# Attention woven into a feed-forward network: ten small pieces a step, all in program order, with new Gram blocks and an inversion over three steps

## The chip, the cores and the metric

The kernel runs on one core of one Trainium2 chip, all in fp32. The metric is device time in microseconds (us); the kernel before takes 770.18 us (median of three runs, 769.65 to 772.47). Engines are named as the profile names them: PE is TensorE's matmuls, PEld its weight loads, DVE is VectorE, ACT is ScalarE, POOL is GpSimd, SP issues the DMAs. A line such as L571 is a line of the kernel that the profile belongs to, so the same operation has another line number in another version; a small table below gives both.

## The reference

Two blocks in a row: a delta-rule attention over 768 positions, and a feed-forward network with a PReLU in the middle.

```python
# q, k, v: (4, 8, 768, 48), beta: (4, 8, 768)
k_n = k / (norm(k) + 1e-6)
for t in range(S):
    y[:, :, t] = q_t @ state
    state = state + beta_t * outer(k_t, v_t - k_t @ state)
x = y.transpose(0, 2, 1, 3).reshape(3072, 384)
h = x @ w_in                                  # 384 -> 2048
g = maximum(h, 0) + alpha * minimum(h, 0)
out = g @ w_out                               # 2048 -> 384
```

The kernel cuts the 768 positions into 12 chunks of 64, and the four batch entries into two pairs, so there are 24 attention steps `n`. In a chunk the recurrence becomes a triangular system per head. Its 64x64 inverse is made from two 32x32 blocks, which VectorE inverts, and two small products on TensorE (`between_1`, `between_2`). The entries of the system come from Gram matrices, the products of a chunk's k with itself and with its q, for which k and q are transposed first (`flips`).

## The kernel before

VectorE inverts the blocks of four steps at once (`eliminate`: 30 pairs of a product and an addition, then two transposes of the whole block). A step of attention has four pieces, and `weave` deals the pieces out among the feed-forward products. PSUM is the memory that TensorE writes its results to. "Filler" is products whose results nobody needs, which keep TensorE busy where it would wait.

```python
BUSY = 31        # filler products ahead of the first groups that need an inverse
EARLY = 6        # Gram matrices are made this many steps ahead

def ps_big():    # three buffers of two PSUM banks, for all attention
    return psum.tile([128, 2, 512], FP32, name="p_big", tag="big", bufs=3)
def ps_one():    # half of such a buffer
    return ps_big()[:, 0]
def ps_ffn():    # two buffers of one bank, for all feed-forward products
    return psum.tile([128, 512], FP32, name="p_ffn", tag="ffn", bufs=2)

def flips(n_k, n_q):                       # transposes of k and of q
    both = n_k < N and n_q < N
    p = ps_big() if both else None         # one tile, two halves
    if n_k < N:
        p_k = p[:, 0] if both else ps_one()
        flip(early(n_k), p_k)              # four TensorE transposes
        ...
        nc.scalar.copy(k_t[n_k]..., p_k)
    if n_q < N:
        p_q = p[:, 1] if both else ps_one()
        flip(q_pad[n_q % NQ], p_q)
        ...
        nc.scalar.copy(q_t[n_q]..., p_q)

def eliminate(m):                          # blocks of steps 4m to 4m + 3
    ...
    for j in range(1, HB - 1):             # 30 pairs on VectorE
        nc.vector.tensor_tensor(out=prod, ..., op=ALU.mult)
        nc.vector.tensor_tensor(out=r[...], in0=r[...], in1=prod, op=ALU.add)
        yield
    nc.vector.transpose(turned[m]..., r)
    nc.vector.transpose(inverse[m]..., r...)
    yield

def attention(n):                          # four pieces
    place(n + 1)                           # ScalarE puts the blocks into diag and inv
    through_state(n)
    yield
    solve(n)
    yield
    outputs(n)                             # and the next state
    between_1(n + 1)
    grams(n + EARLY, n + 1)
    yield
    between_2(n + 1)
    to_ffn(n)
    flips(n + EARLY + 1, n + 2)
    prep(n + EARLY + 1)
    ...                                    # loads of later steps
    yield

# opening, in program order (a manual schedule on all engines): weights, steps 0 to 3
busy(BUSY)
...
weave((eliminate(1), HB), (ffn_out(0, True), OUT_PARTS))
place(NJ); between_1(NJ); between_2(NJ); grams(N, NJ); scale_v(NJ)
opening.close()                            # from here on a scheduler orders the engines

for n in range(NJ, N):
    gens = [(attention(n), 4)]
    if (n + 2) % NJ == 0 and n + 2 < N:
        gens.append((eliminate((n + 2) // NJ), HB))   # a whole inversion in one step
    ...                                    # half a chunk of feed-forward products
    weave(*gens)
```

A feed-forward product is two instructions on TensorE in the profile, a group of 16 quarter-array products of attention is 32 instructions, and a "visit" below is an uninterrupted stretch of attention work between two stretches of feed-forward work.

## Time and profile before

| | before |
|---|---|
| median time | 770.18 us |
| span of the profiled run, granted clock | 767.8 us, 0.982 |
| TensorE busy | 721.8 us, 94% |
| first output product of the feed-forward network | at 150.5 us |
| last one ends (start of its last instruction and 0.32 us) | at 763.4 us |

After 150.5 us TensorE sets the pace. The two costliest rows of the groups of instructions are these (busy time and mean length of one, then the idle time of the engine just before them and what ended the largest part of it):

```profile
L571 PE MATMUL p_ffn<-xt,w_in 128*128 128x256 f32 x1152 | 275.1, 391 | 14.1 <-DVE g L582 6.9
L601 PE MATMUL p_ffn<-w_out,g 128*128 128x384 f32 x768 | 262.2, 494 | 3.8 <-ACT diag L439 2.9
```

TensorE is idle before its wide products for only 14.1 + 3.8 us of 767.8, and what ended the largest part of that (6.9 us) is `g`, the eviction on VectorE (L582).

Line numbers of the operations that are named most:

| operation | before | after |
|---|---|---|
| feed-forward in / out | L571 / L601 | L593 / L623 |
| evict `g` on VectorE | L582 | L604 |
| transposes of k and q (`flips`) | L323 | L327 |
| copy k transposed out of PSUM (`k_t`) | L337 | L341 |
| `between_1`, `between_2` | L463, L476 | L480, L495 |
| filler | L663 | L697 |

### The profile page before, as it was taken

The numbers are of one execution on the slowest core, as the hardware profiler recorded it, in microseconds if no ns is written. First come the engines' busy times: TensorE is split into PE (matmuls) and PEld (weight loads), VectorE is DVE, ScalarE is ACT, GpSimd is POOL, SyncE is SP. The second block draws the span as 40 slices with busy tenths as digits, with TensorE's granted clock in tenths as the row PEclk, the third lists the DMA queues.
The fourth block names the chain that finished last, engine by engine and source line by source line (L and its number), as shares of the span: only waits on it lengthen the run. The fifth ranks groups of instructions, "written<-read, shape, count | busy, mean of one in ns | idle before, by whom it ended". The sixth has DMA issues, their size and how long they took to land.

```text
span 767.8 us, 20517 instructions
## 1 busy us (share of the span) xinstructions
PE 721.8 (94%) x8987; PEld 517.9 (67%) x8987; DVE 412.2 (54%) x979; ACT 251.7 (33%) x563; POOL 21.5 (3%) x80
## 2 busy tenths in 40 slices
PE   5999888898998999998999998999999999999997
PEld 4546666555676678666678667678667677687774
DVE  5886788896599224596224596214596233132020
ACT  3416656514424234125134124123114223021110
POOL 5000000010000000000000000000000000000000
PEclk9999899999999999999999999999999999999999
DMA  6815564311321122121122121111111110100000
GB/s 120 215 39 144 136 175 99 81 25 32 64 47 31 30 43 43 23 42 34 31 43 44 22 43 22 33 32 32 22 33 33 22 35 10 22 12 2 21 0 21
DMA packets 110185, 37.61 MB, mean 49 GB/s; under 512 B 103392, under 2 KB 106480, under 8 KB 110096
## 3 DMA queue, kind: packets, MB, share of 16 engines
q1 hardware_dynamic: 110064, 36.29, 21.7%
q8 instruction: 71, 1.16, 0.6%
q14 instruction: 18, 0.15, 0.1%
q10 hardware_dynamic: 32, 0.01, 0.0%
HBM read 31.56 MB, written 4.72 MB: 47 GB/s over the span
## 4 chain that ended last, share of the span: by engine, by line
PE 57%; DVE 29%; ACT 6%; issue 6%; POOL 1%; DMA 1%; SPq 0%; POOLq 0%; DVEq 0%; ACTq 0%
PE p_ffn L601 24%; PE p_ffn L571 21%; DVE prod L413 7%; DVE block L419 7%; DVE g L582 2%; PE p_big L503 2%; PE p_big L353 2%; PE p_big L530 2%; PE p_big L517 1%; DVE block L399 1%; DVE turned L424 1%; ACT diag L439 1%; DVE inverse L426 1%; DVE kk L359 1%; PE p_big L536 1%
## 5 line engine op out<-in xcount | busy, mean ns | idle before, releaser
L571 PE MATMUL p_ffn<-xt,w_in 128*128 128x256 f32 x1152 | 275.1, 391 | 14.1 <-DVE g L582 6.9
L601 PE MATMUL p_ffn<-w_out,g 128*128 128x384 f32 x768 | 262.2, 494 | 3.8 <-ACT diag L439 2.9
L571 PEld LDWEIGHTS p_ffn<-xt,w_in 128*128 128x128 f32 x1152 | 215.6, 193 | 50.0 <-ACT space_out L202 5.5
L601 PEld LDWEIGHTS p_ffn<-w_out,g 128*128 128x128 f32 x768 | 143.5, 192 | 95.9 <-ACT diag L439 3.2
L582 DVE SCALAR_TENSOR_TENSOR g<-low,al_t,p_ffn 128x256 f32<-128x256 f32 x192 | 83.6, 477 | 127.2 <-ACT low L579 127.1
L579 ACT ACTIVATE low<-p_ffn 128x512 f32<-128x512 f32 x96 | 56.8, 593 | 96.5 <-PE p_ffn L571 88.5
L413 DVE TENSOR_TENSOR prod<-block 128x30 f32<-128x30 f32 (+9 forms) x180 | 59.3, 330 | 5.5
L419 DVE TENSOR_TENSOR block<-block,prod 128x30 f32<-128x30 f32 (+9 forms) x180 | 59.4, 330 | 5.1
L544 DVE TENSOR_TENSOR y<-y,p_big 128x384 f32<-128x384 f32 x22 | 12.1, 552 | 58.8 <-PE p_big L530 58.8
L607 ACT COPY o_sb<-p_ffn 128x384 f32<-128x384 f32 x24 | 11.5, 478 | 90.1 <-PE p_ffn L601 90.1
L663 PE MATMUL p_ffn<-k_t,ident 128*128 128x512 f32 x76 | 37.9, 647 | 0.0
L439 ACT ACTIVATE diag<-inverse,which 64x128 f32<-64x128 f32 (+1 forms) x72 | 28.7, 399 | 23.1 <-PE p_big L476 17.5
L467 ACT COPY mid<-p_big 128x256 f32<-128x256 f32 x24 | 8.8, 372 | 80.1 <-PE p_big L463 80.1
L506 DVE TENSOR_TENSOR r<-v_raw,p_big 128x384 f32<-128x384 f32 x22 | 12.0, 550 | 37.0 <-PE p_big L503 36.8
L481 DVE TENSOR_TENSOR inv<-inv,p_big 128x256 f32<-128x256 f32 x24 | 10.0, 417 | 37.2 <-PE p_big L476 36.5
L439 ACT ACTIVATE inv<-inverse,which 128x256 f32<-128x256 f32 x48 | 21.7, 500 | 24.7 <-PE p_big L517 24.5
L663 PEld LDWEIGHTS p_ffn<-k_t,ident 128*128 128x128 f32 x76 | 14.8, 204 | 16.2 <-issue 15.7
L439 ACT ACTIVATE diag<-turned,which 128x256 f32<-128x256 f32 x24 | 11.6, 506 | 39.5 <-DVE turned L424 39.4
L353 PE MATMUL p_big<-k_t 48*64 48x64 f32 x768 | 18.3, 239 | 6.2 <-ACT k_t L337 4.3
L476 PEld LDWEIGHTS p_big<-diag,mid 64*64 64x64 f32 x768 | 14.3, 141 | 13.7 <-issue 9.8
L306 DVE TENSOR_REDUCE norm<-ksq 128x8 f32<-128x384 f32 x24 | 13.1, 546 | 17.1 <-ACT ksq L304 17.1
L392 ACT ACTIVATE same<-kk,which 128x256 f32<-128x256 f32 x24 | 12.2, 508 | 29.5 <-DVE kk L359 29.4
(94 smaller groups left out, 634.6 us busy)
## 6 DMA issues: line engine op xcount, KB each, us to landing
w_out<-in_moe_w_in_dram SPq DMA_DIRECT2D x12, 512.0 KB, 5.5
qp<-in_q_dram SPq DMA_DIRECT2D x48, 96.0 KB, 2.9
v_raw<-in_v_dram SPq DMA_DIRECT2D x48, 96.0 KB, 2.8
kl<-in_k_dram SPq DMA_DIRECT2D x96, 48.0 KB, 2.7
out_dram<-o_sb SPq DMA_DIRECT2D x48, 96.0 KB, 2.2
ke<-in_k_dram SPq DMA_DIRECT2D x46, 96.0 KB, 3.0
space_out<-in_moe_w_out_dram SPq DMA_DIRECT2D x11, 384.0 KB, 3.7
w_out<-in_moe_w_out_dram SPq DMA_DIRECT2D x5, 384.0 KB, 3.7
```

The costliest lines, as they stand in the source:

```text
L353: nc.tensor.matmul(p[half(t ^ a if w else t), a, w, g], k_t[n][dims(a), g, half(t)], rhs[n][dims(a), g, half(t)],)
L413: nc.vector.tensor_tensor(out=prod, in0=r[:, 0:j, j : j + 1].to_broadcast([128, j, n]), in1=r[:, j : j + 1, j + 1 : HB].to_broadcast([128, ...
L419: nc.vector.tensor_tensor(out=r[:, 0:j, j + 1 : HB], in0=r[:, 0:j, j + 1 : HB], in1=prod, op=ALU.add)
L439: nc.scalar.mul(dst[n % NE][to or rows, a.start * G : a.stop * G, cols], src[m][rows, heads], which[rows, i : i + 1],)
L476: nc.tensor.matmul(p[half(t), a, g], mid[n % 2][half(t ^ a), a * G + g], diag[n % NE][half(t ^ a), a * G + g, HB:C],)
L503: nc.tensor.matmul(p[half(t), a, w, g], x[n][dims(a), g, half(t)], state[bp][dims(a), t, g])
L530: nc.tensor.matmul(p[half(t), a, g], a_t[n][half(t ^ a), a * G + g], us[n][half(t ^ a), a, g])
L571: nc.tensor.matmul(p_h[:, i], w_in[:, t, (f + i) * 128 : (f + i + 1) * 128], xt[:, t], start=(t == 0), stop=(t == KT - 1),)
L579: nc.scalar.activation(low, p_h, ACT.Relu, scale=-1.0)
L582: nc.vector.scalar_tensor_tensor(out=g[:, i], in0=low[:, i], scalar=al_t[:, f + i : f + i + 1], in1=p_h[:, i], op0=ALU.mult, op1=ALU.add,)
L601: nc.tensor.matmul(p_o[bp], gs[f // 2][:, f % 2, bp * 128 : (bp + 1) * 128], w_out[:, f], start=(f == 0), stop=(f == FT - 1),)
L663: nc.tensor.matmul(p, ident, k_t[NJ - 1].rearrange("p g i -> p (g i)"))
```

## The change

The intent is to keep TensorE always supplied: cut a step of attention into ten pieces, so that between two pieces there is a wide product to hide each hop over another engine; spread an inversion over three steps, so that VectorE is never full; make Gram matrices eight steps ahead; and fix the order of every engine by hand for the whole kernel, not for the opening alone.

```diff
-EARLY = 6
+EARLY = 8
+FIRST = 6
-    opening = ExitStack()
-    opening.enter_context(tc.manual_schedule(engines={
+    ctx.enter_context(tc.manual_schedule(engines={
...                                            # grams: kk and two masked gathers become
-            nc.vector.tensor_tensor(out=kk[n_k]..., in0=p[:, :, 0], in1=..., op=ALU.mult)
+            for dst, cols in (                 # two scaled evictions and two copies of 32 rows
+                (gather(n_k), slice(0, HB)), (right[n_k % EARLY][:, 1:], slice(HB, C))
+            ):
+                nc.vector.tensor_tensor(out=dst..., in0=p[:, :, 0, :, cols], in1=w, op=ALU.mult)
...
+    def changes(n):                            # steps up to 4 need fewer placements
+        return n > NJ
...
+    SHARES = 10
     def attention(n):
-        place(n + 1)
+        place(n + 1, (0,))
         through_state(n)
         yield
+        between_1(n + 1)
+        place(n + 1, (1, 2))
+        yield
         solve(n)
         yield
-        outputs(n)
-        between_1(n + 1)
-        grams(n + EARLY, n + 1)
-        yield
-        between_2(n + 1)
-        to_ffn(n)
         flips(n + EARLY + 1, n + 2)
         prep(n + EARLY + 1)
...
+        yield
+        outputs(n)
+        yield
+        between_2(n + 1)
+        scale_v(n + 1)
+        yield
+        next_state(n)
+        yield
+        grams(N, n + 1)
+        yield
+        grams(n + EARLY, N)
+        yield
+        to_ffn(n)
         yield
...
-    opening.close()
...
-        gens = [(attention(n), 4)]
-        if (n + 2) % NJ == 0 and n + 2 < N:
-            gens.append((eliminate((n + 2) // NJ), HB))
+        gens = [(attention(n), SHARES)]
+        if n == NJ:                            # two more Gram matrices, to be eight ahead
+            gens.append((catch_up(), 5 * (EARLY - FIRST) // 2))
+        if n == NJ + 1 or (n % NJ == 0 and NJ + 4 <= n < N - NJ):
+            blocks = eliminate(n // NJ + 1)
+        if n > NJ and n % NJ < 3 and n < N - NJ:
+            share = HB // 2 if n < 2 * NJ else 11
+            gens.append((part(blocks, share), share))
```

More of the change, by code (lines that the diff above doesn't have):

```diff
@@ L290 @@
         nc.gpsimd.memset(t, 0.0)
-    stats, k_t, q_t, kk, a_t = {}, {}, {}, {}, {}
+    right = [const.tile([128, H + 1, HB], FP32, name=f"right{i}") for i in range(EARLY)]
+    for t in right:
+        nc.gpsimd.memset(t[:, 0], 0.0)
+    stats, k_t, q_t, a_t = {}, {}, {}, {}
     def by_parity(x):
@@ L357, in grams @@
         if n_k < N:
-            kk[n_k] = work.tile([128, H, C], FP32, name="kk", bufs=EARLY)
-            nc.vector.tensor_tensor(
-                out=kk[n_k].rearrange("p (a g) i -> p a g i", a=2),
-                in0=p[:, :, 0],
-                in1=stats[n_k][1][:, 0:2, :, None].to_broadcast([128, 2, G, C]),
-                op=ALU.mult,
-            )
+            w = stats[n_k][1][:, 0:2, :, None].to_broadcast([128, 2, G, HB])
+            for dst, cols in (
+                (gather(n_k), slice(0, HB)), (right[n_k % EARLY][:, 1:], slice(HB, C))
+            ):
+                nc.vector.tensor_tensor(
+                    out=dst.rearrange("p (a g) i -> p a g i", a=2), in0=p[:, :, 0, :, cols],
+                    in1=w, op=ALU.mult,
+                )
             keep(n_k)
@@ L385, with gather @@
     same, block, inverse, turned = {}, {}, {}, {}
-    def keep(n):
+    def gather(n):
         m, j = n // NJ, n % NJ
@@ L391, in keep @@
             same[m] = work.tile([128, NJ, H, HB], FP32, name="same", bufs=1)
-        nc.scalar.mul(same[m][:, j], kk[n][:, :, 0:HB], which[:, 0:1])
-        nc.vector.scalar_tensor_tensor(
-            out=same[m][:, j], in0=kk[n][:, :, HB:C], scalar=which[:, 1:2], in1=same[m][:, j],
-            op0=ALU.mult, op1=ALU.add,
-        )
+        return same[m][:, j]
+    def keep(n):
+        m, j = n // NJ, n % NJ
+        for t in range(2):
+            own = slice(64 * t + HB, 64 * t + C)
+            if n < NJ:
+                nc.vector.tensor_copy(out=same[m][own, j], in_=right[n % EARLY][own, 1:])
+            else:
+                nc.scalar.copy(same[m][own, j], right[n % EARLY][own, 1:])
         if j == NJ - 1:
@@ L446, in place @@
         if 1 in parts:
-            put(diag, second, inverse, 1, a=slice(0, 1))
-            for t in range(2):
-                put(diag, second, inverse, 1, half(t), half(1 - t), slice(1, 2))
+            put(diag, second, inverse, 1, a=slice(0, 1 if changes(n) else 2))
+            if changes(n):
+                for t in range(2):
+                    put(diag, second, inverse, 1, half(t), half(1 - t), slice(1, 2))
         if 2 in parts:
             put(inv, first, inverse, 0)
-            put(inv, second, inverse, 1)
+            if changes(n):
+                put(inv, second, inverse, 1)
             w = stats[n][1]
@@ L463, in between_1 @@
             nc.tensor.matmul(
-                p[half(t ^ a), a, g], kk[n][half(t), a * G + g],
+                p[half(t ^ a if changes(n) else t), a, g],
+                right[n % EARLY][half(t), a * G + g : a * G + g + 2].rearrange("p b i -> p (b i)"),
                 diag[n % NE][half(t), a * G + g, 0:HB],
@@ L475, in between_2 @@
         for g, a, t in quarters():
+            x = half(t ^ a if changes(n) else t)
             nc.tensor.matmul(
-                p[half(t), a, g], mid[n % 2][half(t ^ a), a * G + g],
-                diag[n % NE][half(t ^ a), a * G + g, HB:C],
-            )
-        to = inv[n % NE].rearrange("p (a g) i -> p a g i", a=2)[:, :, :, HB:C]
-        nc.vector.tensor_tensor(out=to, in0=to, in1=p, op=ALU.add)
+                p[half(t), a, g], mid[n % 2][x, a * G + g], diag[n % NE][x, a * G + g, HB:C]
+            )
+        to, own = (
+            x[n % NE].rearrange("p (a g) i -> p a g i", a=2)[:, :, :, HB:C] for x in (inv, diag)
+        )
+        nc.vector.tensor_tensor(out=to, in0=to if changes(n) else own, in1=p, op=ALU.add)
     nv, rhs_, ys, us, xts = {}, {}, {}, {}, {}
@@ L532, in outputs @@
             )
-        if c < NCH - 1:
-            p_s = ps_big()[:, :, 0 : G * D].rearrange("p t (g d) -> p t g d", g=G)
-            for g, a, t in quarters():
-                nc.tensor.matmul(
-                    p_s[half(a), t, g], k_late[n % NKL][half(t ^ a), 2 * g + a],
-                    us[n][half(t ^ a), a, g],
-                )
         if c == 0:
@@ L546, in outputs, with next_state @@
             )
+    def next_state(n):
+        c, bp = steps[n]
         if c < NCH - 1:
-            nc.vector.tensor_tensor(out=state[bp], in0=state[bp], in1=p_s, op=ALU.subtract)
+            p = ps_big()[:, :, 0 : G * D].rearrange("p t (g d) -> p t g d", g=G)
+            for g, a, t in quarters():
+                nc.tensor.matmul(
+                    p[half(a), t, g], k_late[n % NKL][half(t ^ a), 2 * g + a],
+                    us[n][half(t ^ a), a, g],
+                )
+            nc.vector.tensor_tensor(out=state[bp], in0=state[bp], in1=p, op=ALU.subtract)
     def to_ffn(n):
@@ L651, in attention @@
         load_v(n + 3)
-        load_late(n + 2)
-        scale_v(n + 1)
+        yield
[5 more added lines that the diff above has]
+        next_state(n)
+        load_late(n + 2)
+        yield
[4 more added lines that the diff above has]
+        to_ffn(n)
         yield
@@ L676, in pair @@
             outputs(i)
+            next_state(i)
             load_late(i + 2)
@@ L794 @@
         (conv_out, PARTS_OUT - 10), (ffn_in(1), IN_PARTS),
-        (statics(2 * NJ, EARLY + 3), 2 * (EARLY + 4 - 2 * NJ) + 1),
+        (statics(2 * NJ, FIRST + 3), 2 * (FIRST + 4 - 2 * NJ) + 1),
     )
-    flips(EARLY + NJ, NJ)
+    flips(FIRST + NJ, NJ)
     flips(N, NJ + 1)
-    prep(EARLY + NJ)
-    load_early(EARLY + NJ + NKE)
+    prep(FIRST + NJ)
+    load_early(FIRST + NJ + NKE)
     load_q(NJ + 2)
@@ L813, in feed_forward, with catch_up @@
             yield from ffn_out(c)
+    def catch_up():
+        for n in range(FIRST + NJ, EARLY + NJ):
+            grams(n, N)
+            prep(n + 1)
+            flips(n + 1, N)
+            load_early(n + 1 + NKE)
+            yield
     tail = feed_forward()
```

## The prediction

> **What bounds the kernel now.** I read the page first: engine shares, the 40 slices, then the costly groups.
>
> ```profile
> PE 721.8 (94%) x8987; PEld 517.9 (67%) x8987; DVE 412.2 (54%) x979; ACT 251.7 (33%) x563; POOL 21.5 (3%) x80
> ...
> PE   5999888898998999998999998999999999999997
> ...
> DVE  5886788896599224596224596214596233132020
> ...
> PEclk9999899999999999999999999999999999999999
> ```
>
> TensorE (PE) is busy 94% of a span of 767.8 us, and from slice 12 on it is nearly always at 9. VectorE (DVE) is heavy in the opening and then in waves: a `596`-like crest every six slices, when a batch of blocks is inverted (180 pairs of products and additions at 330 ns each, 59.3 + 59.4 us in all, plus transposes of 2 us). So after the opening TensorE sets the pace, except on the crests. The end of the chain of waits gives TensorE's undisturbed rate for the two feed-forward products:
>
> ```profile
> 722.25 20.72 PE p_ffn L571 x96
> 742.97 20.66 PE p_ffn L601 x64
> ```
>
> 20.72/96 = 0.2158 us per 128x256 instruction and 20.66/64 = 0.3228 us per 128x384. A chunk is 96 + 64 of them, 41.4 us; twelve chunks, 496.5 us. The last chunk is this tail, which the change leaves alone. The rest of TensorE's time is attention, waits, and changing from one to the other. The last item is in no row of the page; it has to be read off the timeline, from start to start:
>
> ```profile
> 186.95 1.56 PE L601 MATMUL p_ffn<-w_out,g 128*128 128x384 f32 x4
> 188.44 0.68 PE L517 MATMUL p_big<-r,inv 64*64 64x48 f32 x32
> 189.05 1.56 PE L601 MATMUL p_ffn<-w_out,g 128*128 128x384 f32 x4
> 190.54 0.68 PE L530 MATMUL p_big<-u,a_t 64*64 64x48 f32 x32
> ...
> 204.67 0.68 PE L530 MATMUL p_big<-u,a_t 64*64 64x48 f32 x32
> 205.17 0.65 PE L536 MATMUL p_big<-u,kl 64*64 64x48 f32 x32
> 205.64 0.63 PE L463 MATMUL p_big<-diag,kk 64*64 64x32 f32 x32
> ```
>
> Four wide products between two small groups take 190.54 - 189.05 = 1.49 us, not 4 x 0.3228 = 1.29: 0.20 too much. A stretch of 18 or 22 is also 0.20 too long, so this is a charge per stretch, 0.10 for each side that touches a group of quarter-array products. Stretches with transposes on one side show 0.10, with transposes on both about 0. A lone group of 32 takes 189.05 - 188.44 = 0.61 us, but inside a run of groups each takes 0.47 (two 1.08, five 2.49). So one more isolated visit to attention costs 0.20 + 0.14 = **0.34 us**, with nothing waited for.
>
> The waits, on the crest of the inversion:
>
> ```profile
> 455.37 2.83 PE L571 MATMUL p_ffn<-xt,w_in 128*128 128x256 f32 x12 [0.76 <-ACT low L579]
> 458.65 1.10 PE L571 MATMUL p_ffn<-xt,w_in 128*128 128x256 f32 x4 [0.45 <-DVE g L582]
> ...
> 468.82 0.63 PE L323 MATMUL p_big<-ident,ke 128*128 128x128 f32 x4 [0.17 <-DVE a_t L369]
> 470.80 1.96 PE L571 MATMUL p_ffn<-xt,w_in 128*128 128x256 f32 x4 [1.35 <-DVE g L582]
> ```
>
> TensorE waits here for `g`, which stands behind the inversion on VectorE; the last four then run at half speed (1.96 us instead of 0.86), because the clock had dropped.
>
> **What the Trainium skill says.** "TensorE: Matmul & The Clock Gate", Part 3, The mechanism, has it that a weight load passes running matmuls only where the row group differs. A 128x128 load touches every row group, so it should be exposed after quarter products; the trace agrees with a charge at each change, 0.10 us against a load of 0.19, and not after transposes. The same page, Part 1, describes a clock that falls to half when the array has been idle for a window of about 3.4 us; here the granted clock of 460 to 500 us was 0.96, and group L463 took 0.98 us after the 2.76 us wait at 180 us instead of 0.68. "SBUF — State Buffer", SBUF: two separate sides, says that GpSimd and some VectorE operations lock a shared port for a whole instruction. That agrees with:
>
> ```profile
> 8.27 2.10 DVE L308 TENSOR_SCALAR norm<-norm 128x8 f32<-128x8 f32 x1 [0.27 <-ACT norm L307]
> 8.43 1.00 POOL L290 MEMSET inv<- 128x512 f32 x2
> ```
>
> where an operation that takes 0.17 us elsewhere lasts 2.10, until GpSimd's memsets are over.
>
> **The change part by part.**
>
> *Ten pieces.* From the first output product on (150.5 us) I counted both programs' TensorE order. The work is equal: 455.1 us of wide products, 172 groups, 184 transposes. Before, 78 visits to attention and 138 sides; after, 147 and 292. Before: 455.1 + 172 x 0.47 + 184 x 0.11 + 78 x 0.142 + 138 x 0.1 = 581.0 us. It took 613.1 (150.5 to 763.6), so waits and half-clock stretches are 32 us. Going through the stretches one by one finds 30 of them: 4 behind the second inversion (150 to 180), 3.5 in the next 34 us, 22 later. After: 606.2 us. **So the ten pieces cost 25.2 us of TensorE time, on the engine that sets the end**, and pay only by the waits they remove.
>
> *Inversion over three steps.* About 27 us of VectorE in one step, plus about 10 for the rest of that step, exceeds a step of 57.8/2 = 28.9 us; hence the crests. With 11 of 32 parts a step it is 9 + 10 = 19 us, which fits. Three crests of about 5 us and the first one (225 to 250 us, 8 us) should mostly go. What stays: the two closing transposes are contiguous (1.95 + 2.01 us), and two PSUM buffers give TensorE about 3.8 us of slack, so 1.5 to 2 us at each of four endings; about 3 us where ScalarE's burst of placing (2.9 us) holds up `low`; 3 at the dense start, where two steps carry 16 parts each. About 12 us.
>
> *Program order at the hand-over.* The old scheduler put 40 output products ahead of the first group that needs the second inverse; now there are 32. 8 x 0.6456 = 5.2 us less cover. VectorE no longer has three later norms hoisted into that inversion (-2 us). A wait of about 6 us, 1.3 us for a now uncovered hop over ScalarE, and 1.7 us of half clock make 9 against 4 to 5 before. Waits after 150 us: about 21 against 32, a gain of **11 to 12**.
>
> *Gram blocks.* `kk` (682 ns) and two masked gathers (508 on ScalarE, then 483 on VectorE) become two scaled evictions of 256 columns (about 0.33 each, from the pair of L369) and two copies of 32 rows. In the opening this is on the chain: 1.8 us becomes about 1.2, and VectorE no longer waits for ScalarE in the middle. Four times at the start gives -1.9 us, less about 0.8 because eight more memsets prolong the port lock shown above: -1. For blocks 4 to 9, on a VectorE busy 34.2 of 40 us, about -3. Later it is beside TensorE's work.
>
> *Fewer placements for steps 0 to 4.* 1.25 + 0.91 us of ScalarE becomes 0.5 + 0.5. Between 55 and 60 us half is covered by wide filler, -1; at 77 to 82 us, with ScalarE solid, -2. Opening in all: **-7 us**.
>
> Sum: +25 - 12 - 7 = +6; 770 becomes 776. I shade to 775, since the opening has several half-clock stretches (54, 85, 105, 126 us) of which one or two may vanish.
>
> **The rivals.** (1) *Waits vanish*: fine interleaving hides every hop, only the hand-over remains; after-waits of 10, opening -9, time about 755. For it: idle time of TensorE after 260 us is only 10 us, all of it on crests and small. Against: the fixed charge remains, and 32 us is all there was. (2) *VectorE in strict order becomes the wait*: each attention operation heads its queue until TensorE reaches it, `g` stands behind, and two buffers of `p_ffn` are too few; waits stay at 30 us and time is 786 to 790. For it: steps 5 and 6 are close to full on VectorE. Against: 19 us in 28.9 later. (3) *The charge is smaller than I think*, if weight loads for short stretches are pulled ahead: at half of it, 762. Against: four-product stretches before already show the full 0.20.
>
> **Range and chances.** The charge is the surest term (+-4), waits +-6, opening +-4, together about +-8: 762 to 787. Faster by over 2% means under 754.8 and needs rival 1 in full; slower means over 785.6 and needs rival 2.
>
> **What would show it.** After the change, four-product stretches should still run 0.20 us long and lone groups 0.61; about 147 visits; a wait of 5 to 8 us for `diag` before the first group of step 4; no wait over 2 us on later crests; the first wide product about 7 us earlier than 150.5 for L601. A step pair without blocks to invert (53.0 us from 620.8 to 673.8 now) should become longer by about 2 us. I am wrong if those pairs do not lengthen, or if TensorE's waits after the hand-over stay above 20 us.

## The result and the profile after

The changed kernel takes **793.32 us** (median of four runs, 788.95 to 794.42) against 769.91 us for the kernel before in the same rounds. The ratio is 1.0298, with a 95% interval from 1.0251 to 1.0345: slower by 3%. (A ratio here is the mean time of one kernel's fast runs over that of the other's in the same rounds, so it is not quite the ratio of the medians.) The prediction of 775.0 us with a range of 762 to 787 was wrong. All runs gave correct outputs.

The page of the changed kernel, profiled on its fastest run (788.95 us, span 786.9 us), has these lines for the totals and the 40 slices:

```profile
PE 744.7 (95%) x8987; PEld 521.5 (66%) x8987; DVE 404.0 (51%) x987; ACT 251.8 (32%) x564; POOL 22.2 (3%) x88
...
PE   5999988968999999999999999999999999999997
...
DVE  6987888884388336537336537337446223122020
...
PEclk9999999987999999999999999999999999999999
```

TensorE does the same 8987 instructions as before and is busy for 22.9 us more (744.7 against 721.8). The later crests of VectorE went from 9 to 7, as the change meant. Yet the time is longer, so a busier TensorE is not a faster one here. There is one new hole: slices 9 and 10, where the granted clock falls to 8 and 7 tenths.

Waits of TensorE over the whole run, by what it waited for (total, times, longest). First the changed kernel, then the kernel before:

```profile
PE p_big L327 <- ACT k_t L341: 11.2, 12, 3.7
PE p_big L480 <- issue: 7.0, 1, 7.0
...
PE p_ffn L593 <- DVE g L604: 2.3, 2, 2.1
```

```profile
PE p_ffn L571 <- DVE g L582: 6.9, 8, 1.4
...
PE p_ffn L601 <- ACT diag L439: 2.9, 1, 2.9
```

The waits for `g` that the change was made for went from 8 to 2. In their place two others have grown: 7.0 us at once before L480 (2.8 us before, at L463), and twelve waits of a transpose for the copy of `k_t` (three before, 2.1 us in all).

The accounting of the prediction, done on both traces with the same unit costs, gives the whole difference. "Nominal" is what the instructions from the first output product to the last would take in their order, with the charge for each visit and no waits; "excess" is what they took beyond that. An output product "ends" here at the start of its last instruction and 0.32 us.

| us | before | after | difference |
|---|---|---|---|
| first output product starts | 150.5 | 146.2 | -4.3 |
| nominal | 581.0 | 606.2 | +25.2 |
| excess | 31.9 | 30.1 | -1.8 |
| last output product ends | 763.4 | 782.6 | +19.2 |

So the changed kernel pays the 25.2 us of finer interleaving and gets almost nothing back. The excess of 30.1 us lies in four places: 13.5 at the hand-over from the opening to the main loop (146 to 184 us), 5.5 in the next step (189 to 198 us), 8.9 in ten equal places of 0.89, and about 2 everywhere else. Here are the first three in the timeline of the changed kernel (start, length, engine, line, operands, number of instructions, and in brackets the idle time before).

At the hand-over, VectorE ends the second inversion, ScalarE places it, and only then can TensorE go on:

```profile
171.85 1.91 DVE L435 STREAM_TRANSPOSE turned<-block 128x1024 f32<-128x1024 f32 x1
173.79 0.51 ACT L454 ACTIVATE diag<-turned,which 128x256 f32<-128x256 f32 x1 [5.86 <-DVE turned L435]
174.40 1.92 PE L480 MATMUL p_big<-diag,right 64*64 64x32 f32 x32 [6.98 <-issue]
```

The wait of 6.98 us is put down to issue, but the two lines above it show its real end: `diag` is there at 174.30, TensorE starts at 174.40. The group then takes 1.92 us, since the clock had fallen: the same form of it takes 1.12 at full clock (at 51.67 us, shown under e8). That is itself more than the 0.67 of later steps (at 185.26 us); why is told under e9. The same trace in stretches of time shows for how long (columns: us, busy time and instructions of PE, PEld, DVE, ACT and POOL, granted clock, share of the DMA engines, GB/s):

```profile
160.00:170.60 10.60, 7.41 (x23) 4.01 (x22) 9.67 (x28) 0.96 (x2) 0.00 (x0) 1.00 0.13 31
170.60:184.30 13.70, 8.96 (x198) 8.43 (x199) 7.77 (x14) 3.76 (x10) 0.00 (x0) 0.50 0.02 6
```

The granted clock was half for 13.7 us.

In the next step the transposes of q (at 193.88 us) wait 3.70 us for ScalarE to copy the transposed k out of the way. ScalarE's order decides when that is: the copy stands behind a square root, whose argument comes from VectorE, which is held by a transpose of a whole block. The lines of VectorE and ScalarE:

```profile
190.29 1.92 DVE L410 STREAM_TRANSPOSE block<-same 128x1024 f32<-128x1024 f32 x1 [0.88 <-ACT same L407]
...
192.65 0.21 ACT L311 ACTIVATE norm<-norm 128x8 f32<-128x8 f32 x1 [1.85 <-DVE norm L310]
192.77 1.05 ACT L341 COPY k_t<-p_big 128x512 f32<-128x512 f32 x2
```

ScalarE is idle for 1.85 us although the copy could have been done. That is what strict order means for an engine that serves several chains.

The ten equal places, one for each pair of sets of transposes from then on:

```profile
415.02 0.60 PE L327 MATMUL p_big<-ident,ke 128*128 128x128 f32 x4
...
415.66 0.58 ACT L341 COPY k_t<-p_big 128x512 f32<-128x512 f32 x1 [0.42 <-PE p_big L327]
...
416.30 0.66 PE L327 MATMUL p_big<-ident,qp 128*128 128x128 f32 x4 [0.68 <-ACT k_t L341]
```

The four transposes of q wait until ScalarE has copied the transposed k away. They write the other half of the same PSUM tile, another bank, so nothing in the data asks for that; the program orders accesses by tile. The Trainium skill, "PSUM — Partial Sum Buffer", PSUM bank collisions raise a hardware error, asks for semaphores by bank and 32-partition quadrant, and says that two engines on different banks run clean. So with two tiles the wait should go (each then takes one of the three buffers of attention, and uses half of it), and the first experiment tests this. In the kernel before, the scheduler had put 30 instructions of `through_state` between the two sets of transposes in the corresponding place, and waits of this kind come to 2.1 us in all.

### The profile page after: what moved, and what is told of

Read it like the earlier page. It is cut to its first block, busy times and chain, and to the rows that moved or that the text cites. A ratio compares the mean times of both kernels' runs of the same rounds, so it can differ in the third digit from the quotient of the medians.

```text
span 786.9 us, 20530 instructions
## 1 busy us (share of the span) xinstructions
PE 744.7 (95%) x8987; PEld 521.5 (66%) x8987; DVE 404.0 (51%) x987; ACT 251.8 (32%) x564; POOL 22.2 (3%) x88
## 4 chain that ended last, share of the span: by engine, by line
PE 77%; DVE 15%; ACT 5%; issue 2%; POOL 1%; POOLq 0%; DVEq 0%; ACTq 0%
PE p_ffn L623 31%; PE p_ffn L593 28%; PE p_big L357 3%; DVE prod L424 3%; DVE block L430 3%; PE p_big L523 3%; PE p_big L327 2%; PE p_big L495 2%; PE p_big L550 2%; PE p_big L537 2%; PE p_big L566 2%; DVE g L604 2%; PE p_big L480 2%; ACT k_t L341 1%; DVE inverse L437 1%
## 5 line engine op out<-in xcount | busy, mean ns | idle before, releaser
L593 PE MATMUL p_ffn<-xt,w_in 128*128 128x256 f32 x1152 | 284.6, 392 | 4.9 <-DVE g L604 2.3
L623 PE MATMUL p_ffn<-w_out,g 128*128 128x384 f32 x768 | 271.5, 497 | 0.4 <-DVE g L604 0.3
L604 DVE SCALAR_TENSOR_TENSOR g<-low,al_t,p_ffn 128x256 f32<-128x256 f32 x192 | 83.5, 476 | 134.9 <-ACT low L601 134.9
L407 ACT COPY same<-right 32x256 f32<-32x256 f32 x40 | 16.1, 402 | 84.0 <-DVE right L366 83.8
L375 DVE TENSOR_TENSOR a_t<-p_big,minus 128x256 f32<-128x256 f32 x48 | 17.9, 419 | 28.1 <-PE p_big L357 28.1
L310 DVE TENSOR_REDUCE norm<-ksq 128x8 f32<-128x384 f32 x24 | 13.2, 548 | 30.2 <-ACT ksq L308 30.1
L480 PEld LDWEIGHTS p_big<-diag,right 64*64 64x64 f32 x768 | 16.4, 138 | 16.3 <-issue 14.0
L480 PE MATMUL p_big<-diag,right 64*64 64x32 f32 x768 | 18.9, 224 | 7.8 <-issue 7.0
L327 PE MATMUL p_big<-ident,qp 128*128 128x128 f32 x96 | 15.5, 293 | 11.2 <-ACT k_t L341 11.2
L454 ACT ACTIVATE diag<-inverse,which 64x128 f32<-64x128 f32 (+2 forms) x62 | 25.4, 410 | 2.0 <-DVE inverse L437 1.3
L357 PEld LDWEIGHTS p_big<-k_t 48*64 48x64 f32 x768 | 16.0, 156 | 13.3 <-issue 6.9
L580 ACT COPY xt<-p_big 128x384 f32<-128x384 f32 x24 | 11.2, 477 | 42.6 <-PE p_big L579 42.4
```

What stands on the lines that cost most here:

```text
L327: nc.tensor.transpose(p[:, g * 128 : (g + 1) * 128], src[:, 2 * g : 2 * g + 2].rearrange("p h d -> p (h d)"), ident,)
L357: nc.tensor.matmul(p[half(t ^ a if w else t), a, w, g], k_t[n][dims(a), g, half(t)], rhs[n][dims(a), g, half(t)],)
L454: nc.scalar.mul(dst[n % NE][to or rows, a.start * G : a.stop * G, cols], src[m][rows, heads], which[rows, i : i + 1],)
L480: nc.tensor.matmul(p[half(t ^ a if changes(n) else t), a, g], right[n % EARLY][half(t), a * G + g : a * G + g + 2].rearrange("p b i -> p ( ...
L593: nc.tensor.matmul(p_h[:, i], w_in[:, t, (f + i) * 128 : (f + i + 1) * 128], xt[:, t], start=(t == 0), stop=(t == KT - 1),)
L604: nc.vector.scalar_tensor_tensor(out=g[:, i], in0=low[:, i], scalar=al_t[:, f + i : f + i + 1], in1=p_h[:, i], op0=ALU.mult, op1=ALU.add,)
```

## The experiments

Fourteen runs (no run has the number e5): the theories after the result were that the charge per visit is real (e12 measures it alone; that it makes up the loss is the accounting above), and that three repairable waits, which the change itself had made, hide the gain (e1, e4, e8). The rivals were that four pieces would keep the gain without the charge (e2, e7), that program order is the loss (e6), and that the Gram blocks gain by themselves (e9, e13, e14). In the diffs "-" is the kernel that is named in the text. Gram matrices eight steps ahead, fewer placements in steps 0 to 4, and ten pieces under the old scheduler were not tried alone.

| run | what | us, median | ratio to before | first output product | nominal | excess |
|---|---|---|---|---|---|---|
| before | | 769.91 | 1 | 150.5 | 581.0 | 31.9 |
| after | the change | 793.32 | 1.0298 | 146.2 | 606.2 | 30.1 |
| e1 | two PSUM tiles | 780.12 | 1.0119 | 144.0 | 606.2 | 18.4 |
| e2 | four old pieces | 788.89 | 1.0208 | 151.6 | 581.2 | 51.8 |
| e3 | inversion in one step | 827.57 | 1.0730 | 152.6 | 606.2 | 67.5 |
| e4 | cover at the hand-over | 786.22 | 1.0196 | 151.3 | 606.2 | 28.0 |
| e6 | before, in program order | 825.41 | 1.0726 | 147.7 | 581.3 | 88.9 |
| e7 | four new visits, two tiles | 781.22 | 1.0153 | 145.1 | 579.4 | 47.4 |
| e8 | filler | 788.45 | 1.0244 | 145.9 | 606.2 | 30.0 |
| e9 | before with the new blocks | 776.21 | 1.0069 | 152.5 | 581.4 | 36.6 |
| e10 | six pieces and all repairs | 765.05 | 0.9919 | 144.7 | 590.6 | 24.7 |
| e11 | ten pieces and all repairs | 773.68 | 1.0035 | 144.9 | 606.2 | 15.5 |
| e13 | e9 and filler | 771.36 | 1.0023 | 153.3 | 581.4 | 36.3 |
| e14 | before and filler | 768.14 | 0.9983 | 148.9 | 581.0 | 28.9 |
| e15 | e10, transposes apart | 763.02 | 0.9909 | 144.6 | 590.6 | 23.9 |

The last three columns are of the one profiled run of each, which may be a run faster or slower than the median.

### e1_two_tiles: the shared PSUM tile

```diff
 # the changed kernel, in flips
-        both = n_k < N and n_q < N
-        p = ps_big() if both else None
+        both, p = False, None
```

> The changed kernel with one edit: the transposes of k and of q in one piece go to two PSUM tiles instead of the two halves of one. Theory (the second set waits for ScalarE's copy of the first because both lie in one tile): the eight transposes take 0.9 us instead of 1.77 in nine steps (-8 us), and up to 3 us of the 4.8 us at step 4 go; 781 to 785 us, ratio to before about 1.016. Rival (the wait only moves on, to the three PSUM buffers of attention or to the next group): unchanged, 791 to 795 us.

Measured: 780.12 us (775.07 to 782.68), ratio 1.0119 [1.0075, 1.0162], so 13 us came back for two lines, a little more than I expected. The transposes now follow each other at once:

```profile
403.86 0.60 PE L327 MATMUL p_big<-ident,ke 128*128 128x128 f32 x4
404.30 0.60 PE L327 MATMUL p_big<-ident,qp 128*128 128x128 f32 x4
```

0.44 us from start to start instead of 1.28, and no idle time. The excess fell from 30.1 to 18.4 us, by 11.7, where the ten places and the 3.9 us in step 4 add up to 12.8. So the wait came from the shared tile, and it was the program's own.

### e2_four_pieces: the old pieces in the new order

```diff
 # the changed kernel: SHARES = 4, and attention in the four pieces of the kernel before
-    SHARES = 10
+    SHARES = 4
...
         solve(n)
         yield
+        outputs(n)
+        next_state(n)
+        between_1(n + 1)
+        grams(n + EARLY, n + 1)
+        yield
+        between_2(n + 1)
+        to_ffn(n)
         flips(n + EARLY + 1, n + 2)
```

> The changed kernel with the step of attention in four pieces again, as before, but still in program order, with three-step inversion and Gram matrices eight ahead. Theory of the charge (0.34 us for each isolated visit): 79 visits and 138 sides instead of 147 and 292, TensorE's sum 581 instead of 606, so -25 us: 768 us give or take 4, ratio about 1.00. Rival (ten pieces are what hides the hops between engines; with four, waits return): 780 us or more, with single waits of TensorE over 1 us in most steps.

Measured: 788.89 us (782.72 to 790.96), ratio 1.0208 [1.0154, 1.0262]. The charge of 25 us went (nominal 581.2), but 22 us of excess came in its place (51.8 against 30.1): after 150 us TensorE waits 7.3 us in twelve places before the Gram products (L357), and 9.9 us in eight before wide products, for `g` or `low`. The rival was mostly right. In program order the ten pieces do what they are meant for; they cost about as much as they hide.

### e3_one_step: a whole inversion in one step

```diff
 # the changed kernel, main loop
-        if n == NJ + 1 or (n % NJ == 0 and NJ + 4 <= n < N - NJ):
-            blocks = eliminate(n // NJ + 1)
-        if n > NJ and n % NJ < 3 and n < N - NJ:
-            ...
+        if (n + 2) % NJ == 0 and n + 2 < N:
+            gens.append((eliminate((n + 2) // NJ), HB))
```

> The changed kernel with the inversion of later batches in one step again (in the steps where the kernel before has it). Theory (the three-step spread is what removed the crests' waits): +12 to +20 us, 805 to 813 us, ratio about 1.05, with waits of TensorE for g in steps 6, 10, 14 and 18. Rival (ten pieces in program order hide the inversion anyhow): at most 797 us.

Measured: 827.57 us (824.85 to 832.60), ratio 1.073 [1.0673, 1.0788], more than I expected. The excess is 67.5 us, 37 more than with three steps, and the waits for `g` come to this:

```profile
PE p_ffn L593 <- DVE g L604: 17.6, 11, 2.5
```

against 2.3 us in two waits with three steps (of each, one wait of 2.1 to 2.2 us lies in the opening). The rest is 10 us of waits for `diag`, and half clock. Spreading the inversion is worth 34 us in program order.

### e4_cover: more output products behind the second inversion

```diff
 # the changed kernel
-    weave((eliminate(1), HB), (ffn_out(0, True), OUT_PARTS))
+    late, ahead = ffn_out(1), 12
+    weave((eliminate(1), HB), (chain(ffn_out(0, True), part(late, ahead)), OUT_PARTS + ahead))
...                                            # steps 4 and 5 get 10 of them each, in place of 16
```

> The changed kernel with 12 of the 32 output products of chunk 1 issued behind chunk 0's, under the second inversion, and 10 instead of 16 in each of steps 4 and 5. Theory (the 7.0 us wait before the first group of step 4, and the half clock after it, are lost time that program order brought): -7 to -10 us, 783 to 786 us, ratio about 1.018. Rival (the products are then missing as filler in steps 4 and 5, which wait instead): 790 us or more.

Measured: 786.22 us (783.51 to 791.79), ratio 1.0196 [1.0137, 1.0255]; the profiled run is the slowest of the four. The excess at the hand-over fell from 13.5 to about 3 us. But step 4 has less cover now, its transposes wait 4.77 us for the copy of `k_t`, and the clock falls to half there for 13.7 us (195.6 to 209.3). So both expectations are partly right: the hole can be filled, and it reopens in the next step until the shared tile goes too.

### e6_before_in_order: the kernel before without its scheduler

```diff
 # the kernel before
-    opening = ExitStack()
-    opening.enter_context(tc.manual_schedule(engines={
+    ctx.enter_context(tc.manual_schedule(engines={
...
-    opening.close()
```

> The kernel before with nothing changed but that the rest too is in program order. Theory (the scheduler hid hops between engines that program order with four pieces exposes, as in e2, and the inversion in one step then stands in front of everything on VectorE): waits of 60 us or more instead of 32, 800 to 825 us, ratio 1.04 to 1.07. Rival (the scheduler's order was worth little, and what made the changed kernel slower is the charge alone): 770 to 785 us.

Measured: 825.41 us (822.49 to 828.64), ratio 1.0726 [1.0686, 1.0765], with an excess of 88.9 us instead of 31.9. Program order alone exposes 57 us, which the scheduler had hidden by moving work across pieces. So the other parts (ten pieces, three steps) make good some 33 of the 56 us that program order costs (by the ratios).

### e7_regrouped: four visits in the new order

```diff
 # the changed kernel with two tiles (e1): SHARES = 4 and six yields fewer
         place(n + 1, (0,))
         through_state(n)
-        yield
         between_1(n + 1)
         place(n + 1, (1, 2))
         yield
         solve(n)
-        yield
         flips(n + EARLY + 1, n + 2)
...                       # outputs, between_2 and next_state together; both grams and to_ffn together
```

> Two tiles for the transposes as in e1, and the step of attention in four visits of at most three PSUM buffers each, no two of a visit depending on each other: state and first block product; solve and transposes; output, second block product and next state; both Gram products and the transposes of y. Theory (the charge per visit is real, and the waits of e2 came from putting five groups, more than the three buffers, into one visit): TensorE's sum 579 instead of 606, waits as in e1 (18 us), so about 26 us under e1's 780: 754 to 760 us, ratio 0.98. Rival (any coarse step in program order brings back hops of VectorE and ScalarE): waits of 35 us or more, 772 us or more.

Measured: 781.22 us (777.57 to 785.80), ratio 1.0153 [1.0104, 1.0203]. The nominal time is the lowest of all, 579.4 us, and the excess 47.4 takes it back. TensorE waits for `g` again, although no visit has more than three groups of quarter products:

```profile
PE p_ffn L622 <- DVE g L603: 13.9, 9, 2.1
```

My theory (754 to 760) fell; the rival was right. Neither way of making four visits that was tried (e2, e7) is free of such waits; why `g` is late here was not taken apart.

### e8_filler: three more filler products

```diff
 # the changed kernel
-BUSY = 31
+BUSY = 34
```

The profiled run of the changed kernel is 4 to 5 us faster than its other four. The program with the dummy groups (e12, below) has the same instructions up to 746 us and was profiled on an ordinary run, so the two can be laid side by side in the opening, at the first groups that need an inverse. First the fast run, then the ordinary one:

```profile
51.67 1.12 PE L480 MATMUL p_big<-diag,right 64*64 64x32 f32 x32
53.64 1.12 PE L480 MATMUL p_big<-diag,right 64*64 64x32 f32 x32 [0.85 <-DVE a_t L375]
```

```profile
49.30 1.12 PE L480 MATMUL p_big<-diag,right 64*64 64x32 f32 x32
53.67 1.92 PE L480 MATMUL p_big<-diag,right 64*64 64x32 f32 x32 [3.24 <-DVE a_t L375]
```

In both, the second group can start at 53.6 us, when the mask `a_t` frees its buffer. In the ordinary run the filler was over 2.4 us earlier, so TensorE waited 3.24 us instead of 0.85, and the clock fell. From 55 us on, in the ordinary run:

```profile
55.00:58.00 3.00, 3.00 (x24) 1.43 (x21) 0.00 (x0) 2.28 (x7) 0.00 (x0) 0.50 0.64 179
58.00:62.00 4.00, 4.00 (x42) 2.43 (x42) 1.45 (x3) 0.58 (x3) 0.00 (x0) 0.50 0.01 5
```

TensorE is busy all the time and its clock stays at half, for 13.7 us in all; the first output product comes at 150.6 instead of 146.2 us.

> The changed kernel with 34 instead of 31 filler products in the opening. Theory (the 7 us by which the openings of the traces differ come from the clock: where the filler runs at full clock early, it ends before VectorE has the first inverse, TensorE idles 3.5 us and the clock is halved for up to 17 us): every run falls near the short opening, median 787 to 790 us instead of 793, spread under 4 us, and no half clock between 52 and 70 us. Rival (the openings differ for another reason): median and spread as before, 793 us and 5 us or more.

Measured: 788.45 us (787.47 to 789.36, five runs), ratio 1.0244 [1.0214, 1.0273]. In the profiled run there is no half clock from 52 to 70 us and the first output product is at 145.9, and the spread between runs shrinks to 2 us. Theory right: the 4 to 5 us between runs are this wait and the half clock after it.

### e9_blocks_only, e14_before_filler and e13_blocks_filler: the Gram blocks alone

```diff
 # e9: the kernel before (scheduler, four pieces, one-step inversion, EARLY = 6) with only
 # the new grams, gather, keep, changes, place and between_1 / between_2 of the change
 # e14: the kernel before with BUSY = 34;  e13: e9 with BUSY = 34
-BUSY = 31
+BUSY = 34
```

> The kernel before, with the old scheduler, four pieces, one-step inversion and six ahead, and only the new form of the Gram blocks (two scaled evictions, copies of 32 rows, right tiles, fewer placements for steps 0 to 4). My prediction put this at -7 us: 763 us, ratio 0.991. Now I think that half of it is lost to the clock in the opening: -4 to 0, ratio 0.995 to 1.000. If the forms themselves cost something later (longer work on ScalarE), ratio over 1.005.

e9 measured: 776.21 us (770.27 to 777.29), ratio 1.0069 [1.0028, 1.0111]. The profiled run has half clock from 54.7 us for 13.7 us and its first output product at 152.5. So the blocks alone gain nothing; they cost 0.7%.

One cost of theirs is in no term of the prediction. Where there are fewer placements (steps 0 to 4), each of the two small products, by its code, lets its 32 instructions use two of the four quarters of the array instead of four. From its first to its last start such a group takes 0.90 us at full clock (eight groups between 51.67 and 83.58 us in the changed kernel), and 0.45 in the kernel before and in the steps after. That is 0.45 us for each of ten groups, eight of them in the opening. How much of it reaches the time is not shown.

To see whether a gain is there and the clock eats it, the last two:

> The kernel before with 34 filler products instead of 31 ahead of the first groups that need an inverse; nothing else. Its profile shows TensorE idle for 1.84 us there and one half-clock window of 3.4 us (54.5 us on). Three products more (0.44 us each, 1.3 us) should swallow most of that wait. If the filler is worth something only where the wait ahead of the mask is about 3.5 us, as after the change, this kernel gains nothing: 769 to 771, first output product at 150 to 151. If the filler alone is a gain whatever the Gram blocks, it gains 3 us or more: 764 to 767.

> The kernel before with the new Gram blocks alone (as the run of the blocks only, 776.2 us) and 34 filler products instead of 31. My theory: the new blocks do shorten the opening by some 4 to 6 us, but the shorter chain lets TensorE run into a wait that halves the clock for 13 to 17 us and gives it back; with the filler the first output product comes at 145 to 147 instead of 152.5, and the time is 768 to 771, so 1 to 3 us under the kernel before with the same filler, since the waits after the opening stay 36 us against 32. Rival: the blocks' gain in the opening is not real, the first output product stays at 150 or later and the time above 773.

e14 measured 768.14 us (764.99 to 771.26), ratio 0.9983 [0.9955, 1.001]: between the two expectations, and not told apart from no gain. e13 measured 771.36 us (770.14 to 777.21), ratio 1.0023 [0.9993, 1.0052]. Five of its six runs lie between 770.14 and 771.79; the profiled one was the sixth, 777.21, and even 34 fillers were too few there (a wait of 1.18 us at 53.55, half clock for 13.7 us from 55.0, first output product at 153.3). So the filler is worth 3.5 to 5 us to the blocks (by the ratios 1.0069 and 1.0023, or by the medians), about as I thought. But with it they still do not beat the kernel before with the same filler: they are 3 us behind. In the profiled runs the excess after the opening is 36.3 us against 28.9. My theory (1 to 3 us ahead) is not borne out, and neither is the rival's "above 773" for the median. Whether the blocks shorten the opening of an ordinary run of e13, with the loss all later, stays open, as none of those runs was profiled.

### e10_six_fixed and e11_ten_fixed: all repairs, with six pieces and with ten

```diff
 # both: two tiles (e1), cover of 12 (e4), BUSY = 34 (e8).  e10 has in addition
-    SHARES = 10
+    SHARES = 6
...                       # visits: [through_state] [between_1] [solve, flips]
...                       # [outputs, between_2] [next_state, gram of q] [gram of k, to_ffn]
```

> All three mends (two tiles, 12 products as cover for the second inversion, 34 filler products) and the step of attention in six pieces of one or two groups, so that a visit never asks for more than two PSUM buffers of quarter products. Theory (the charge is paid per visit, waits come only where a visit holds several groups with one chain or buffers run out): TensorE's sum 590.6 us from the first output product (606.2 in ten pieces), waits of 10 to 14, opening 146: 750 to 758 us, ratio 0.98. Rival (fewer, longer stretches of wide products make TensorE wait for g at once): over 765 us.

> The three mends with the ten pieces kept. Theory: the sum stays 606.2, of the 30 us of waits 8 go with the tiles and about 10 at the hand-over, opening 146 in every run: 766 to 770 us, ratio 0.997, that is, the ten pieces with all their waits mended only draw level with the kernel before. Rival (the mends do not add up, since the wait at the hand-over moves into step 4): 774 us or more.

e11 measured 773.68 us (771.63 to 775.81), ratio 1.0035 [1.0009, 1.006]: with every wait repaired that I had found, the ten pieces only come near the kernel before and stay 0.1 to 0.6% behind. Its excess is 15.5 us, half that of the kernel before, and its nominal time is 25.2 us more. e10 measured **765.05 us** (762.79 to 766.34), ratio 0.9919 [0.9897, 0.9941], so it beats both kernels, though it is 7 us over the end of what I expected (750 to 758), and at the edge of the rival's "over 765". Against the kernel before with the same filler (e14, 0.9983, in other rounds) the lead is 0.6%. It has 15.6 us less to pay than ten pieces and 9 us more of waits. Two of those are at the ends of inversions:

```profile
353.55 1.96 DVE L434 STREAM_TRANSPOSE turned<-block 128x1024 f32<-128x1024 f32 x1
...
355.37 1.98 DVE L436 STREAM_TRANSPOSE inverse<-block 128x1024 f32<-128x1024 f32 x1
...
358.00 0.81 ACT L406 COPY same<-right 32x256 f32<-32x256 f32 x2 [5.75 <-DVE right L365]
...
359.85 0.87 DVE L603 SCALAR_TENSOR_TENSOR g<-low,al_t,p_ffn 128x256 f32<-128x256 f32 x2 [1.89 <-ACT low L600]
...
360.87 4.08 PE L592 MATMUL p_ffn<-xt,w_in 128*128 128x256 f32 x10 [1.74 <-DVE g L603]
```

(Lines have lower numbers here than in the changed kernel, L603 for L604.) VectorE does about 3.8 us of transposes in one piece. Its Gram evictions (L365) come after them, ScalarE's copy (L406) has waited 5.75 us for these, and `low` and so `g` stand behind that copy. TensorE is idle for 1.74 us, and ten instructions take 4.08 us, most of it at half clock, instead of 2.2.

### e15_six_apart: the two closing transposes one part apart

```diff
 # e10, in eliminate (and one part more where parts are counted)
         nc.vector.transpose(turned[m]..., r)
+        yield
         inverse[m] = ...
```

> The six-piece version that beat both kernels (765.05 us), with the two closing transposes of an inversion one part apart (33 parts in place of 32) instead of back to back, so that the waiting evictions get between them. Theory: the two waits for g of 3.7 us (at 358 and 473 us), and the half clock after each, come from 4 us of transposes in one piece; apart, each costs at most 0.5 us and the time is 756 to 761. Rival: the waits come from the sum of VectorE's work on that step and only move; time 763 to 766.

Measured: **763.02 us** (761.50 to 765.78), ratio 0.9909 [0.9884, 0.9935], the lowest median of all. In this trace the transposes stand 5.22 us apart (358.30 and 363.52), and no wait for `g` over 0.7 us is left between 300 and 700 us; the excess of the two stretches of 50 us that held those waits (from 350 and from 450 us) went from 7.6 us to about 2.4. The gain in time is smaller than the theory's, and since e10 and e15 ran in different batches, their two intervals overlap: e15 may be better by up to about 4 us, or not at all. In its profiled run the excess only moved: 13.6 us of half clock in two windows between 190 and 228 us, where e10's has 3.4. That part is the rival's.

### e12_charge: the charge by itself

```diff
 # the changed kernel; the last chunk has no attention beside it
+    for n, _ in enumerate(tail):
+        if n % 4 == 3 and n < 44:
+            dummy()                        # 11 lone groups, four input products between them
+        if n == 63:
+            for _ in range(11):
+                dummy()                    # 11 groups in one run, among output products
```

> The charge by itself: the changed kernel with 22 groups of 32 quarter products, whose results nobody reads, put into the last chunk, where no attention is left and nothing is waited for: 11 of them one by one between four input products each, 11 in one run in the middle of the output products. Theory (0.20 us for a stretch between two groups and 0.14 for each lone group): the input part takes 20.7 + 11 x 0.81 = 29.6 us, the output part 20.7 + 11 x 0.47 + 0.34 = 26.2 us. Rival (what I took for a charge is the waits of attention): both parts take 25.9 us.

Measured: one look, 811.19 us. Eleven groups apart, in the timeline (the first of eleven; eight instructions are four products):

```profile
746.12 1.89 PE L593 MATMUL p_ffn<-xt,w_in 128*128 128x256 f32 x8
747.94 0.68 PE L877 MATMUL p_big<-state,inv 64*64 64x48 f32 x32
```

From 746.12 to the first output product at 775.75 are 29.63 us for 96 instructions and 11 groups. Worked out: 96 x 0.2158 + 11 x (0.47 + 0.142 + 2 x 0.10) = 20.7 + 8.9 = 29.6. Nothing waits for data here, so the charge is shown by itself, and the estimate fits to 0.1 us. Eleven groups in one run took more than expected, because of two idle times:

```profile
789.80 2.08 PE L877 MATMUL p_big<-state,inv 64*64 64x48 f32 x128 [1.00 <-issue]
793.28 1.14 PE L877 MATMUL p_big<-state,inv 64*64 64x48 f32 x61 [1.39 <-issue]
```

29.0 us against 26.2; without the 1.00 and 1.39 it is 26.6. The profile names no other engine for these pauses, and what makes them is not shown.

## Why the prediction was wrong

**The step that failed is the sum of the waits after the first output product.** It was to fall from 32 us to 21 and came to 30.1; the opening, put at -7 us, gained 4.3 us at best. The paragraphs below take the terms one by one.

**The charge of 25.2 us was right.** Nominal time grew by 25.2, stretches still run 0.20 us long and lone groups 0.60 to 0.63, and e12 gives the charge alone to within 0.1 us. The late pair of steps that I named as a test, 53.0 us before, takes 55.3 (from 636.6 to 691.9 us): 2.3 longer, predicted about 2. The reason given for the charge is another matter. If a full-array load were exposed because it touches every row group, it should be exposed after transposes too, which are full-array work, and there the traces show about 0. The runs show the charge and not its cause.

**The crests went, more fully than I said.** Of the 12 us that I left for endings, placements and the dense start, the endings and placements, some 9, came to about 2. e3 shows what spreading is worth: 34 us in this order.

**The hand-over was seen but mis-sized.** I said 9 us ("a wait of about 6 us, 1.3 us for a now uncovered hop over ScalarE, and 1.7 us of half clock"). It measured 13.5. The wait (7.0) and the hop (0.95) were near; the half clock was not. I took it to last one short window, as at 180 us in the kernel before, and it lasted 13.7 us here. TensorE was busy for 9.0 us of them, so it lost about 4.5 us where I had 1.7. The slower form of step 4's two small products (told under e9) makes some 0.9 more. The dense start cost 5.5 instead of 3, and not by `g` standing behind VectorE's work, as I thought: 3.9 of it is the chain over ScalarE's copy of `k_t` that was shown above.

**The wait that cost most is in no term of the sum.** I read the kernel before for its long waits, and the sum has nothing for the wait of transposes for `k_t`, 2.1 us in three places. That it was small was the work of the scheduler, and the change takes the scheduler away. In program order the two halves of one PSUM tile wait for each other in every step: 8.9 us in ten places, and e1 gave back 11.7 of excess (with the wait of step 4).

**The opening did not gain 7 us.** In the profiled run it gained 4.3, in ordinary openings nothing (150.6 in e12 and 151.3 to 152.6 in e2, e3 and e4, which have the same opening, against 150.5), because the shorter chain lets TensorE idle (3.24 us in e12) and the clock then stays at half for 13.7 to 17.1 us. e8 shows it: with three fillers more, the first output product is at 145.9 and the runs agree within 2 us. The further claim, that the blocks themselves shorten the kernel, has no support: e9 and e13 gained nothing over their partners.

The whole, for the profiled run: 769.6 - 4.3 + 25.2 - 1.8 = 788.7, and it took 788.95. An ordinary run adds about 5.

**Rival 2's number was near and its reason wrong.** It had said waits of 30 us and a time of 786 to 790, with VectorE in strict order as the cause; the waits came to 30.1, by other causes, and the time to 793.3, of which the profiled run's 788.95 is the low end. After 250 us TensorE waits for `g` for 0.5 us in all, so VectorE did not hold up the wide products; strict order on VectorE did harm in one place, step 4, and there through ScalarE's queue. Rival 1 failed since the charge remains, as its own "against" said. Even e11, with the known waits repaired, does no better than the kernel before.

What stays open: why half clock lasts 3.4 us in one place and 13.7 to 17.1 in another (in all sixteen traces every such stretch that ends before the kernel does is one to five times 3.41 us); the 3 us by which the new blocks fall behind with the filler; whether ten pieces would pay under the old scheduler; and what causes the charge.

## What to carry to other kernels

Finer interleaving has a fixed price on the engine that sets the end; measure the price of one more visit from start to start in the trace (0.34 us here), multiply by the visits added, and compare it with the waits that are there to be removed before anything else. When a scheduler is replaced by program order, every small wait in the old trace has to be asked again, "what stood beside it?", above all tiles whose halves are written by one engine and read by another. A middle grain with the waits repaired one by one (six pieces, 763 to 765 us) beat the coarse kernel by 0.8 to 0.9% and the fine one by more.

## What the Trainium skill lacked or had wrong

- "TensorE: Matmul & The Clock Gate", Part 1, What's actually happening: it has the clock fall after at least one idle window of about 3.4 us, and return to full after at least one busy one. Here it fell after shorter waits as well: at 55.0 us in e13 after one of 1.18 us, with TensorE busy for 2.2 of the 3.4 us before. And one busy window was not enough: waits of 3.24 us (e12's opening) and 6.98 us (hand-over) were both followed by 13.7 us of half clock, in the first case with TensorE busy for the whole of 55 to 62 us; after 1.18 us (e13) it was 13.7 too, and after 2.76 us in the kernel before 3.4. The work in the long cases was quarter-array groups, with filler products of 128x512 between them in the openings. Which of these decides is not shown.
- No page has a figure for changing between full-array and quarter-array work ("TensorEngine Tiling (Array Packing)", Key Properties, says that a change of tiling mode drains TensorE, without one). In fp32 a lone group of 32 instructions among wide products costs 0.34 us over its own 0.47 (e12: 29.63 us measured, 29.6 worked out).
- No page has a case like the pauses of 1.00 and 1.39 us in a run of 352 quarter-array instructions (e12), put down to issue.
- "PSUM — Partial Sum Buffer" has the rule by bank and quadrant, and e1 agrees with it: two banks in one tile cost 0.84 us each time (1.28 against 0.44 us from one set of transposes to the next) only because the program ordered the whole tile. No page warns of that.
